# Another order of the same 1100 steps on every engine: gated mix of a long convolution and a token-shift MLP

## The chip, the cores and the metric

The kernel runs on one core of one Trainium2 chip. The metric is the time of one execution on the device in microseconds. Five engines of the core have instruction streams of their own: PE (matmul), DVE (vector), ACT (scalar), POOL (GpSimd) and SP, which here only issues DMAs. Each engine runs its own instructions in the order in which the program gives them; semaphores make an instruction wait for data from another engine or for a buffer to come free.

## The reference

All inputs are bf16; q, k, v are 1 x 2048 x 640, and x is q.

```
a = q * (irfft(rfft(kv, 4096) * rfft(ssm_k, 4096))[:2048] + kv * ssm_D),  kv = k_shift * v
k_shift[s] = sum over t < 4 of k[s - (3 - t)] * shift_k[:, 3 - t] (per channel)
h  = gelu(layernorm(x) @ w1)           # 640 -> 640
hs = shift(h) @ w2                     # four channel groups, moved by +1, -1, +2, -2 tokens
x1 = x + hs
b  = x1 + gelu(layernorm(x1) @ w3) @ w4   # 640 -> 1536 -> 640
g  = sigmoid(sum(x * gate_w))
out = g * a + (1 - g) * b
```

## The kernel before

Tokens are split over 16 tiles of 128 rows. The MLP works in four chunks (c = 0 to 3) of four tiles: `x_stats` and `x_norm` make the layernorm, `x_turn` transposes the chunk (on PE for chunks 0 and 1, by one DMA_TRANSPOSE issued from SP, line 648, for chunks 2 and 3), `mlp1.c.u` (line 703) is five matmuls of 512 columns into one PSUM bank with a gelu on ACT behind them, `h_shift` and `h_tile` move the tokens, `w2` (line 785) adds the second product to x. `x1_norm.c` makes the second layernorm; its step 6 issues the DMA_TRANSPOSE into the tile x1t. `w3.c.f` (line 837) and `w4.t` (line 864) are the wide MLP.

The long convolution is a Fourier transform of 4096 points done as matmuls, both for kv and for ssm_k. `tap` (line 586) makes k_shift on PE; DVE multiplies it with v into KV (lines 598, 601). `step1` (line 419) is the first transform of KV and of the filter (HT0); its results are cast from PSUM to a staging tile `stg` (lines 356 on ACT, 358 on DVE) and stored to DRAM (S_x, S_h; steps 15 and 16 of each step1, line 433). `gather.x.s` and `gather.h.s` (line 440) read them back, permuted, into tiles `ax`; `step2` (line 461) is the second transform, `product` the complex product on DVE, `step3` (line 508) the inverse, stored to S_g and read by `gin`, and `step4` (line 890) the last transform, joined with the gate and with b. `load_h` loads parts of ssm_k, `load_gw` the gate's weights.

PSUM has 8 banks of 2 KB per partition, shared by all these matmuls. A helper's steps can be emitted one by one; the letters in a step's name (as in `step1.KV.3.AAAVAVAAAV:9`) say for each PSUM evacuation whether ACT (A) or DVE (V) does it:

```
    def evac(ev, dst, src):
        if ev == "A":
            A.copy(out=dst, in_=src)
        else:
            V.tensor_copy(out=dst, in_=src)
```

The order of all engines is one list, `ORDER`, of 1100 entries `helper.arguments.engines:k`, and `emit` executes the k-th step of the named helper, inside `tc.manual_schedule`, which keeps the order as given. So each engine's stream is the list cut to what that engine does; SP's stream (some 100 DMA-issuing steps) is cut from the same list, and all its DMAs go into one hardware queue. `SLOTS` gives for each allocation of a shared ring (tag c: the PSUM banks; row, gt, xt, gq, ax, hp: SBUF rings of 3 or 4 tiles, xt of 2) which buffer it takes; an allocation waits until the last user of that buffer is through.

Of the kernel before, what the change touches and what calls it, by code (L numbers as in the profile page):

```python
# [41 lines left out]
def kernel(  # L42
# [24 lines left out]
        "c": "012345670124703510347205142356401723605162370514731057423671045261304732641374153670421350627413"  # L67
             "502634751264351270361427503164257364102546173045621537426107432715604371401362570164301257613045"
             "267236057416537621507362651374026372401534762501373150427102547535706432073125640736450750634127"
             "504763270415367204325170635147630125460327156034215760147362304167135620316425031672301402715320"  # L70
             "1724107361761423564023714053627501267420674256271306234",
        "row": "01230213021302320123012031203120310310303",
        "gt": "012301031010231012301201",
        "xt": "010101",
        "gq": "0120201201021020120122102121021021",
        "ax": "0123120312030213",
        "hp": "01231302",
# [798 lines left out]
    def step4(t1, ev):  # L876
# [26 lines left out]
        def total():  # L903
# [170 lines left out]
                 f1_table=f1_table, t2_table=t2_table, i_tables=i_tables, f4_table=f4_table, kv_alloc=kv_alloc, k_load=k_load, k_wrap=k_wrap, v_load=v_load, tap=tap,  # L1074
# [51 lines left out]
```

## Time and profile before

| | us |
|---|---|
| median of 3 executions | 229.26 |
| lowest, highest | 227.95, 229.72 |
| span of the profiled execution (first to last instruction) | 225.9 |
| PE busy | 217.5 |
| DVE busy | 192.4 |
| ACT busy | 173.0 |
| POOL busy | 16.3 |
| PE's granted clock, mean | 0.999 |

The profile gives no time of its own for the profiled execution beside its span; the median of the three executions stands 3.4 us above that span. In a row of the profile `out<-in` names the tiles, `xN` is the number of instructions, and the figure behind the comma the mean length of one in ns. Rows of a chain or a timeline begin with start and length in us. PE's 217.5 us count each matmul from its start to a modelled end.

### The profile page before, as it was taken

Reading aid. Unit: us, or ns where it says so; the run is one execution under the profiler, and the core shown is the slowest. Engines: PE = TensorE matmul, PEld = TensorE weight load, DVE = VectorE, ACT = ScalarE, POOL = GpSimd, SP = SyncE. Lnnn points to the kernel's source line nnn. Section 1 sums busy time; section 2 is a strip of 40 time slices with the busy share of each in tenths; the row PEclk is TensorE's granted clock in tenths of the full one; section 3 lists DMA queues with packets and bytes.
Section 4 is the critical chain, followed back from the end, with each engine's and each line's share of the span. In section 5 each row is a group of like instructions: output and inputs, shape, how many; then the busy total and the mean of one; then the engine's idle time right before and its main releaser. Section 6 shows DMA issues by size and latency. Waiting matters only on the chain.

```text
span 225.9 us, 6037 instructions
## 1 busy us (share of the span) xinstructions
PE 217.5 (96%) x2419; PEld 120.4 (53%) x2420; DVE 192.4 (85%) x500; ACT 173.0 (77%) x344; POOL 16.3 (7%) x34
## 2 busy tenths in 40 slices
PE   8979989999999999999999999999999999999994
PEld 2557555436846554344664445555533547657762
DVE  7899999999999999873999998989999841439994
ACT  4799988989989989999977597967988450266450
POOL 3238020000000200010400000000000000000000
PEclk9999999999999999999999999999999999999999
DMA  6999997964998999999999560592695779418915
GB/s 238 381 362 336 308 249 193 344 282 104 392 352 353 307 240 290 376 361 369 300 250 303 121 232 4 156 361 70 69 323 195 219 269 372 189 30 321 310 77 197
DMA packets 43841, 57.62 MB, mean 255 GB/s; under 512 B 20514, under 2 KB 36514, under 8 KB 43558
## 3 DMA queue, kind: packets, MB, share of 16 engines
q1 hardware_dynamic: 43238, 54.62, 75.3%
q0 software_dynamic: 576, 2.62, 3.1%
q8 instruction: 19, 0.31, 0.6%
q14 instruction: 8, 0.07, 0.1%
HBM read 34.94 MB, written 18.36 MB: 236 GB/s over the span
## 4 chain that ended last, share of the span: by engine, by line
PE 63%; DMA 16%; DVE 15%; issue 1%; ACT 1%; SPq 1%; ACTq 0%
PE ps L864 23%; PE ps L837 18%; DMA WA<-in_B_w_dram 5%; DMA W<-in_B_w_dram 5%; PE ps L461 4%; PE ps L890 4%; PE psw L785 4%; PE psm L703 4%; DMA ax<-S_x 4%; PE ps L508 3%; DMA S_h<-stg 3%; PE ps L419 2%; DVE KV L601 2%; DVE KV L598 2%; DVE HT L358 2%; DVE HM L758 1%
## 5 line engine op out<-in xcount | busy, mean ns | idle before, releaser
L837 PE MATMUL ps<-x1t,W 128*128 128x512 bf16 x240 | 56.1, 380 | 0.0
L864 PE MATMUL ps<-W,gt 128*128 128x320 bf16 (+2 forms) x383 | 55.1, 299 | 0.6 <-DMA W<-in_B_w_dram 0.5
L864 PEld LDWEIGHTS <-gt 128*128 128x128 bf16 x384 | 36.2, 98 | 18.3 <-issue 2.8
L841 ACT ACTIVATE gt<-ps 128x512 bf16<-128x512 f32 x48 | 27.6, 609 | 19.0 <-PE ps L864 10.6
L837 PEld LDWEIGHTS <-W 128*128 128x128 bf16 x240 | 21.8, 98 | 28.2 <-issue 5.5
L356 ACT CAST stg<-ps 128x512 bf16<-128x512 f32 x55 | 28.6, 608 | 3.0 <-PE ps L419 1.8
L867 DVE SCALAR_TENSOR_TENSOR X<-ps,OMG,X 128x320 bf16<-128x320 f32 (+2 forms) x32 | 17.2, 548 | 11.9 <-PE ps L864 11.7
L703 PE MATMUL psm<-xt,WA 128*128 128x512 bf16 x100 | 23.4, 379 | 1.2 <-DMA WA<-in_B_w_dram 1.1
L356 ACT CAST gs<-ps 128x320 bf16<-128x320 f32 x41 | 15.6, 439 | 8.7 <-PE ps L508 5.2
L785 PE MATMUL psw<-WA,HT 128*128 128x320 bf16 x116 | 21.3, 299 | 0.2
L358 DVE CAST XS<-ps 128x512 bf16<-128x512 f32 x19 | 12.5, 684 | 5.3 <-PE ps L461 5.3
L356 ACT CAST hs<-ps 128x512 bf16<-128x512 f32 x28 | 15.0, 606 | 1.9 <-PE ps L461 1.9
L358 DVE CAST stg<-ps 128x512 bf16<-128x512 f32 x25 | 15.9, 683 | 0.2
L703 PEld LDWEIGHTS <-WA 128*128 128x128 bf16 x100 | 9.2, 97 | 12.0 <-DMA WA<-in_B_w_dram 1.2
L785 PEld LDWEIGHTS <-HT 128*128 128x128 bf16 x116 | 10.9, 98 | 7.7 <-issue 4.1
L894 ACT ACTIVATE y<-ps,GS 128x320 bf16<-128x320 f32 x22 | 10.4, 526 | 5.7 <-PE ps L890 3.5
L788 DVE SCALAR_TENSOR_TENSOR X<-psw,X 128x320 bf16<-128x320 f32 x32 | 14.2, 483 | 0.1
L358 DVE CAST gs<-ps 128x320 bf16<-128x320 f32 x23 | 10.7, 485 | 2.4 <-PE ps L508 1.7
L706 ACT ACTIVATE HT<-psm 128x512 bf16<-128x512 f32 x20 | 11.6, 618 | 1.2 <-PE psm L703 1.1
L356 ACT CAST XS<-ps 128x512 bf16<-128x512 f32 x21 | 11.9, 609 | 0.5 <-PE ps L461 0.3
L785 PE MATMUL psw<-WA,HM 128*128 128x320 bf16 x44 | 12.3, 299 | 0.0
L794 ACT ACTIVATE jk<-X 128x640 bf16<-128x640 bf16 x16 | 12.1, 759 | 0.0
(145 smaller groups left out, 334.8 us busy)
## 6 DMA issues: line engine op xcount, KB each, us to landing
S_x<-stg SPq DMA_DIRECT2D x8, 640.0 KB
S_h<-stg SPq DMA_DIRECT2D x8, 640.0 KB, 3.4
ax<-S_x SPq DMA_DIRECT2D x8, 640.0 KB, 8.1
ax<-S_h SPq DMA_DIRECT2D x8, 640.0 KB, 6.0
S_g<-gs SPq DMA_DIRECT2D x8, 640.0 KB, 3.6
W<-in_B_w_dram SPq DMA_DIRECT2D x2, 1920.0 KB
kn<-in_A_k_dram SPq DMA_DIRECT2D x4, 640.0 KB
E<-in_A_ssm_k_dram SPq DMA_DIRECT2D x5, 512.0 KB
```

The costliest lines, as they stand in the source:

```text
L356: A.copy(out=dst, in_=src)
L358: V.tensor_copy(out=dst, in_=src)
L703: PE.matmul(ps[:].rearrange("p (a b) -> p a b", a=4), lhsT=W1N[:, k, 160 * u:160 * u + P] if u < 4 else W1M[:, k, :], rhs=xt[:, :, k, :], ...
L706: A.activation(out=st["HT"][:, 4 * c:4 * c + 4, u, :], in_=ps[:].rearrange("p (t b) -> p t b", t=4), func=ACT.Gelu_apprx_tanh)
L785: PE.matmul(ps[:], lhsT=h_tile(f, t1), rhs=W2P[:, f, o:o + W], start=(f == 0), stop=(f == 4))
L788: V.scalar_tensor_tensor(out=X1[:, t1, o:o + W], in0=box["ps"][:], scalar=1.0, in1=X[:, t1, o:o + W], op0=ALU.mult, op1=ALU.add, accum_out ...
L794: A.activation(out=jk[:], in_=X1[:, t1, :], func=ACT.Square, accum_out=S12[:, 1, t1:t1 + 1])
L837: PE.matmul(ps[:].rearrange("p (a b) -> p a b", a=4), lhsT=st["W3"][:, k, f * P:(f + 1) * P], rhs=xt[:, :, k, :], start=(k == 0), stop=(k ...
L841: A.activation(out=st["gt", c, f // 4][:, f % 4, :], in_=ps[:], func=ACT.Gelu_apprx_tanh)
L864: PE.matmul(ps[:], lhsT=st["gt", c, f // 4][:, f % 4, i * P:(i + 1) * P], rhs=st["W4"][:, f, o:o + w], start=(f == 0), stop=(f == FC - 1))
L867: V.scalar_tensor_tensor(out=X1[:, t1, o:o + w], in0=box["ps"][:], scalar=OMG[:, t1:t1 + 1], in1=X1[:, t1, o:o + w], op0=ALU.mult, op1=ALU ...
L894: A.activation(out=box["y"][:], in_=box["ps"][:], func=ACT.Copy, scale=GS[:, t1:t1 + 1])
```

## The change

`ORDER` and `SLOTS` are replaced. The new list has the same 1100 steps, and the functions are unchanged. What differs is the order of the steps on every engine, SP's DMAs among them; the letters of 13 kinds of helper (for instance step1 of KV 27 A and 13 V before, 28 and 12 after; step2.x 21 and 19, then 24 and 16; step3 41 and 23, then 47 and 17; step4 22 and 10, then 18 and 14; x1_norm 6 and 10, then 4 and 12); and the buffer of each ring allocation. Of the ORDER part only lines with steps that are spoken of below are shown.

```
 
     SLOTS = {
-        "c": "012345670124703510347205142356401723605162370514731057423671045261304732641374153670421350627413"
-             "502634751264351270361427503164257364102546173045621537426107432715604371401362570164301257613045"
-             "267236057416537621507362651374026372401534762501373150427102547535706432073125640736450750634127"
-             "504763270415367204325170635147630125460327156034215760147362304167135620316425031672301402715320"
-             "1724107361761423564023714053627501267420674256271306234",
-        "row": "01230213021302320123012031203120310310303",
-        "gt": "012301031010231012301201",
-        "xt": "010101",
-        "gq": "0120201201021020120122102121021021",
-        "ax": "0123120312030213",
-        "hp": "01231302",
+        "c": "012320145673270641524072103647534126427016104237162507437023645136502746354127057402136401357106"
+             "425302745643750173654120350314267513254062045163704376510246135640172306537062145302153674315647"
+             "021573204612071646023754256473017436520705126343625710471235120734653140302037541671403515146730"
+             "203764154176364715207256413501267412104673540721631524075162727270653672451610237161617024172037"
+             "2061401020273030712031264056170261340360431746012350450",
+        "gt": "001110203320201301201302",
+        "row": "00123133312013021320132320302021231021013",
+        "xt": "011101",
+        "gq": "010020110012022012201201021",
+        "ax": "0123130213022301",
+        "hp": "01232031",
     }
     taken = {}
 
@@ -906,169 +906,175 @@
...
-        "k_load.3.AVA:2 load_x.3:0 x_norm.0.VVAA:2 x_stats.1.VVVV:1 k_load.3.AVA:3 x_turn.0.AAA:0 k_load.3.AVA:6 "
-        "k_load.2.VAV:5 load_w1.1:0 x_norm.0.VVAA:3 k_load.2.VAV:1 x_stats.1.VVVV:2 x_turn.0.AAA:1 x_stats.1.VVVV:3 "
...
-        "x_norm.3.VVVV:0 x_norm.3.VVVV:1 k_load.0.AAV:4 load_cj:0 k_load.0.AAV:2 mlp1.1.2:1 x_norm.3.VVVV:2 "
...
-        "mlp1.1.4:0 x_turn.3.D:0 kv_consts:0 x_stats.2.VVAA:2 mlp1.1.0:0 k_load.2.VAV:2 k_wrap:0 k_load.1.AVV:6 "
...
-        "tap.3.VAVA:7 z_cols:0 mlp1.1.1:1 load_gw:0 tap.4.VAAV:5 tap.4.VAAV:3 mlp1.3.1:0 tap.3.VAVA:2 x_stats.2.VVAA:7 "
...
-        "x_turn.2.D:0 h_shift.3:0 tap.0.AVAA:0 tap.2.AVAA:3 tap.2.AVAA:7 tap.2.AVAA:5 tap.3.VAVA:8 mlp1.3.3:0 "
...
-        "mlp1.3.2:1 load_h.1:0 mlp1.2.2:0 tap.0.AVAA:8 tap.2.AVAA:1 tap.1.VAVA:7 h_shift.1:1 tap.0.AVAA:2 load_h.3:0 "
...
-        "step2.x.3.AVVVVVAAVA:8 load_w4:0 w3.0.1:1 scale_x1.4.V:0 step2.x.0.VAVVAVAAVA:12 w3.0.2:1 w3.0.8:1 "
...
-        "step2.x.0.VAVVAVAAVA:4 step2.x.3.AVVVVVAAVA:13 gather.h.6:0 step2.x.0.VAVVAVAAVA:13 x1_norm.1.VVAA:4 "
...
-        "w4.3:2 step2.h.3.AAVVVVAVAA:2 x1_norm.1.VVAA:6 scale_x1.2.A:0 step2.h.3.AAVVVVAVAA:7 step2.h.3.AAVVVVAVAA:8 "
...
-        "w3.1.5:0 w3.1.6:0 step2.h.0.AAVAAAAAVA:10 step2.h.0.AAVAAAAAVA:11 step2.h.0.AAVAAAAAVA:5 step3.7.AAAAAVAV:0 "
...
-        "gather.x.2:0 x1_norm.2.AVVV:4 w4.0:2 w3.1.5:1 w3.1.9:0 x1_norm.2.AVVV:5 w3.1.2:1 product.1:3 product.1:4 "
...
-        "x1_norm.3.AVAA:2 w3.1.3:0 scale_x1.11.A:0 step3.1.VAAVVVAA:6 w3.1.0:0 x1_norm.2.AVVV:6 w3.1.10:0 "
...
...
+        "load_w1.1:0 mlp1.0.2:0 x_norm.1.VVVA:0 x_norm.1.VVVA:1 x_turn.1.VVA:0 x_norm.1.VVVA:2 load_x.3:0 "
...
+        "x_stats.3.VVAA:7 x_norm.3.VVVV:0 mlp1.1.3:1 x_norm.3.VVVV:1 x_norm.3.VVVV:2 x_norm.3.VVVV:3 x_turn.3.D:0 "
...
+        "tap.3.VVVA:4 x_stats.2.VVAA:4 x_stats.2.VVAA:5 tap.3.VVVA:8 tap.3.VVVA:6 mlp1.3.0:0 mlp1.3.0:1 "
...
+        "tap.1.AAVV:2 x_turn.2.D:0 load_h.4:0 step1.KV.3.VAVAVAAAVV:11 tap.1.AAVV:3 z_cols:1 z_cols:2 tap.1.AAVV:6 "
+        "tap.1.AAVV:4 step1.KV.3.VAVAVAAAVV:10 mlp1.2.4:0 mlp1.2.4:1 h_shift.0:1 h_shift.0:2 load_w2:0 mlp1.2.0:0 "
...
+        "step2.x.0.AVAVVVAAVV:0 load_w4:0 step2.x.0.AVAVVVAAVV:2 step2.x.3.VAVVAAAAVA:0 step2.x.3.VAVVAAAAVA:7 "
...
+        "step2.h.3.VVVVAAVAVA:13 gather.h.6:0 step2.h.3.VVVVAAVAVA:9 step2.h.3.VVVVAAVAVA:11 "
...
+        "step2.h.0.AAAAAAAAAV:2 product.7:0 w2.14:4 step2.h.0.AAAAAAAAAV:5 product.7:1 product.7:2 pow0:0 w4.2:3 "
+        "product.7:3 step2.h.0.AAAAAAAAAV:1 gather.x.2:0 product.7:4 gather.h.3:0 w4.3:0 step2.h.0.AAAAAAAAAV:11 "
...
+        "step3.7.AAVAAAAA:2 step3.7.AAVAAAAA:3 product.1:0 product.1:1 product.1:2 product.1:3 x1_norm.1.VVVV:6 "
+        "w3.1.0:0 step3.7.AAVAAAAA:1 w3.1.0:1 step3.7.AAVAAAAA:5 w3.1.8:0 product.1:4 step3.7.AAVAAAAA:9 "
...
+        "x1_norm.2.VVVA:5 gather.x.3:0 step2.x.1.AAAVAAVAAA:12 step2.x.1.AAAVAAVAAA:6 product.0:0 "
...
+        "w3.1.7:0 w3.1.7:1 x1_norm.2.VVVA:6 w3.2.2:0 w3.2.2:1 step2.h.1.AAVVAAAVVA:6 step2.h.1.AAVVAAAVVA:7 "
...
```

306 rows, old and new, of the table ORDER are left out of this document.

## The prediction

> **What bounds the kernel now.** I read the page first, for the shares.
>
> ```profile
> span 225.9 us, 6037 instructions
> PE 217.5 (96%) x2419; PEld 120.4 (53%) x2420; DVE 192.4 (85%) x500; ACT 173.0 (77%) x344; POOL 16.3 (7%) x34
> ```
>
> PE is busy for 217.5 of 225.9 us. The change keeps every PE instruction, so it can win no more than PE's 8.4 us of idle time, and lose as much as it likes. The windows of 10 us show where those 8.4 us lie (columns: PE, PEld, DVE, ACT, POOL busy, granted clock, DMA share, GB/s).
>
> ```profile
> 0.00:10.00 10.00, 8.92 (x38) 3.75 (x39) 7.88 (x41) 5.65 (x9) 3.53 (x15) 1.00 0.80 303
> 10.00:20.00 10.00, 8.22 (x87) 5.51 (x85) 9.65 (x31) 9.95 (x18) 4.28 (x5) 1.00 1.06 354
> 20.00:30.00 10.00, 9.52 (x186) 6.22 (x187) 9.44 (x35) 9.99 (x21) 2.32 (x4) 1.00 1.00 289
> 30.00:40.00 10.00, 9.77 (x262) 5.66 (x252) 9.60 (x36) 8.00 (x17) 1.32 (x2) 1.00 0.87 238
> 40.00:50.00 10.00, 9.42 (x127) 3.66 (x116) 9.52 (x27) 8.94 (x18) 0.00 (x0) 1.00 0.80 302
> 60.00:70.00 10.00, 9.69 (x71) 5.00 (x68) 9.84 (x30) 9.13 (x16) 0.00 (x0) 1.00 0.95 365
> 100.00:110.00 10.00, 9.49 (x84) 5.29 (x85) 5.69 (x16) 9.84 (x24) 0.52 (x1) 1.00 1.06 368
> 110.00:120.00 10.00, 10.00 (x182) 6.23 (x181) 9.41 (x19) 8.49 (x15) 1.89 (x4) 1.00 1.13 257
> 180.00:190.00 10.00, 10.00 (x88) 5.46 (x87) 3.78 (x9) 2.88 (x6) 0.00 (x0) 1.00 0.85 309
> 220.00:226.00 6.00, 2.75 (x22) 1.52 (x20) 2.77 (x7) 0.00 (x0) 0.00 (x0) 0.95 0.54 200
> ```
>
> PE's idle time is 1.1 us in the first window, 1.8 in the second, 2.1 in the five others shown up to 110 us, and 3.25 behind 220, the tail. From 110 on PE is full. DVE is at 9.4 to 9.8 of 10 in the windows of 10 to 70 us: there PE runs at the pace at which DVE empties PSUM and builds operands. After 110 us a new order can win nothing in PE, only lose.
>
> The chain that ended last says the same (start us, length us, what): a weight load, DVE work in the first half, a DMA of W4, then PE alone.
>
> ```profile
> 3.55 11.11 DMA WA<-in_B_w_dram
> 14.65 0.05 issue
> 14.70 3.41 PE psm L703 x15
> ...
> 43.56 0.34 DVE KV L598
> 43.94 0.61 PE ps L419 x4
> 44.55 1.19 PE psm L703 x5
> ...
> 94.93 10.73 DMA W<-in_B_w_dram
> 105.66 0.05 issue
> 105.71 5.06 PE ps L864 x36
> ...
> 222.12 1.02 DVE X L867 x2
> ```
>
> **The change part by part.** Steps, instructions and DMAs are the same; four things move.
>
> *Engines of the evacuations.* The prices:
>
> ```profile
> L356 ACT CAST stg<-ps 128x512 bf16<-128x512 f32 x55 | 28.6, 608 | 3.0 <-PE ps L419 1.8
> L358 DVE CAST stg<-ps 128x512 bf16<-128x512 f32 x25 | 15.9, 683 | 0.2
> L356 ACT CAST gs<-ps 128x320 bf16<-128x320 f32 x41 | 15.6, 439 | 8.7 <-PE ps L508 5.2
> L358 DVE CAST gs<-ps 128x320 bf16<-128x320 f32 x23 | 10.7, 485 | 2.4 <-PE ps L508 1.7
> ```
>
> Counting the letters in the step names, step1 and step2 send 4 casts of 512 columns from DVE to ACT (step1 +1 and +1, step2.x +3, step2.h -1): DVE -4 x 0.683 = -2.7 us, ACT +4 x 0.608 = +2.4. step3 sends 6 casts of 320 columns: DVE -6 x 0.485 = -2.9, ACT +6 x 0.439 = +2.6. The small moves in the taps, norms, transposes and step4 go both ways and stay under 2 us per engine in sum. DVE thus loses some 5 us of work and ACT gains some 3. The step3 part lies where PE is full (after 110 us): worth nothing. The 512-column part lies where DVE sets the pace.
>
> To say what it is worth I add up, in list order and with the durations of rows like these, the work of each engine ahead of every PE step, and take the largest amount by which the DVE work it needs exceeds PE's own: that much PE must stand idle. In the first 100 us this lead is 7.9 us before (at step2.x.3) and 5.0 after. So the DVE-paced stalls should shrink by 7.9 - 5.0 = **2.9 us**. The rows allow it only just: idle PE between 10 and 110 us is about 3.9 (1.8 + 2.1), plus slow spots between kinds that busy time hides. I take -2.9 and keep 0 as the other end.
>
> *Start.* On SP's queue the loads went k.3, x.1, k.2, x.3, w1.1, w1.0; now k.0 and k.1 stand ahead of w1.1, and x.3 behind it. w1.1, which landed at 14.65, thus has one 640 KB load more ahead of it, about 1.85 us at the 354 GB/s of the window 10 to 20; I take 1.6, as it is issued a little earlier. x.3 comes later by more than that. PE has 1.9 us more of k and x transposes listed ahead of the first mlp1 step, which fill that wait. Sum 0; the ends are +1.6 (nothing hides it) and -1.1 (PE's only long wait for a weight goes):
>
> ```profile
> PE psm L703 <- DMA WA<-in_B_w_dram: 1.1, 1, 1.1
> PE ps L864 <- DMA W<-in_B_w_dram: 0.5, 1, 0.5
> ```
>
> *The two DMA transposes of the first layernorm* (x_turn.3.D and x_turn.2.D). The last normalising run ahead of the first of them (from the chain; it ends at 24.16), the issue times, and the first matmuls that need chunk 2:
>
> ```profile
> 23.00 1.16 DVE xn L660 x3
> 24.18 3.43 SPq L648 DMA_TRANSPOSE xt<-xn  x1
> 34.45 2.81 SPq L648 DMA_TRANSPOSE xt<-xn  x1
> ```
> ```profile
> 30.77 4.48 PE L703 MATMUL psm<-xt,WA 128*128 128x512 bf16 x20
> 40.72 2.33 PE L703 MATMUL psm<-xt,WA 128*128 128x512 bf16 x10
> ```
>
> No row gives their landing. The bounds: not before the issue itself is through (2.81 and 3.43 us), and not after the first use (40.72 - 34.45 = 6.3 us). Like sizes in the list of DMA issues (KB, median us to landing) lie between:
>
> ```profile
> S_h<-stg SPq DMA_DIRECT2D x8, 640.0 KB, 3.4
> ax<-S_x SPq DMA_DIRECT2D x8, 640.0 KB, 8.1
> ax<-S_h SPq DMA_DIRECT2D x8, 640.0 KB, 6.0
> ```
>
> I take 5.6, near the 6.0 row, since the queue is full there (DMA share 1.00 and 0.87). For chunk 3 the last x_norm moves 1.6 to 2.7 us later on DVE (1.6 us more DVE work stands ahead of it, and its x arrives later), so the issue moves to about 26.9 and the landing to 32.3. The first step that reads it, mlp1.3.0, has 2.1 us less PE work ahead of it than mlp1.3.1 had; PE gets there at about 30.4. Stall 1.9 (ends 0 and 3.7). For chunk 2, the DVE work ahead is 0.4 us more and its first reader, mlp1.2.4, stands 2.0 us of PE work earlier; PE is 1.9 late by then, DVE partly too, since its taps wait for PE's: stall 1.4 (ends 0 and 2). Also load_h.1, load_h.2, gate weights and load_h.0 are now issued ahead of that transpose. Behind each waiting mlp1 step on PE stand the tap matmuls that feed DVE, so DVE loses the time as well. Sum of both: **+3.3 us** (0 to 5.7).
>
> [...]
>
> *Second half.* PE's list changes kind 6 times more often after 110 us; a change of kind costs about 0.07 us, worked out from the chain's rows:
>
> ```profile
> 120.29 2.16 PE ps L837 x10
> 122.45 0.41 PE ps L508 x16
> 122.86 2.26 PE ps L837 x10
> ```
>
> (2.26 against 2.16 for the same ten matmuls is 0.1 at a change.) That is +0.4 us (0 to 0.6). Three transfers get less cover. gather.h.6 is issued behind step2.x.0's first step, which leaves PE 3.9 us of work before its reader, where the rows above have 3.4 to 6.0 for this size; at their middle, 4.7, and with 0.3 of changes of kind between, +0.5 us (0 to 2.1). x1_norm.1's transpose of the second layernorm (tile x1t) now stands on SP behind gather.x.2 and gather.h.3, which wait until step2.h.3 has freed their buffers, though the data is ready long before; its landing and its first reader, w3.1.0, come out at the same time: +0.3 (0 to 2). x1_norm.2's stands behind gather.x.3 in the same way: +0.3 (0 to 1). Together **+1.5 us** (0 to 5.7). Nothing hides these: PE is full there and its queue is in order. If SP waits, what it has queued behind (the later gathers) is late too. This is the queue's row:
>
> ```profile
> SPq L440 <- PE ps L461: 22.5, 5, 11.0
> ```
>
> *Tail.* After PE's last matmul the same steps follow as before, so the 3.25 us stay. [...]
>
> **Sum:** 0 (start) + 3.3 - 2.9 + 1.5 = +1.9 us. The profiled execution shows a span of 225.9; the median of the three runs, 229.26, is 3.4 above it, and I take those 3.4 us outside the span as unchanged. So 229.26 + 1.9 = **231.2 us**. The case's own range takes ±1.5 to 2: 229.3 to 232.6.
>
> **The rivals.**
>
> *1. The new waits compound.* One SP queue carries everything; each late wait holds back what is queued behind it, and step1.HT0.0's staging reuses the buffer of HT0.1, whose store stands behind two gathers, so ACT may stop there too. Upper halves of the bounds: early 4.2, second half 2.8, DVE-paced gain 2.9: +4.1, 233.3. For: the 22.5 us that SP's queue already waits in the row above. Against: ACT has 1 to 2 us of slack per window at 30 to 50 us.
>
> *2. Other side: the DVE relief stays and the transposes are early enough.* It is one mechanism: x_norm.3's chain keeps its place in time (DVE's lead at the start is smaller too), and the transposes land in 3.4 us as the S_h store does. Then chunk 3 lands at 26.9 + 3.4 = 30.3, ahead of PE's 30.4, the early stall is at most 0.5, the second half costs the 0.4 of switches, and the sum is 0.5 - 2.9 + 0.4 = -2.0: 227.3. It decides at a landing within 3.5 us of issue, or an issue before 24.8. For: DVE really sheds its casts in the windows where it is at 9.6. Against: the queue is fuller there than where the 3.4 was measured.
>
> *3. Nothing to be measured.* PE is 96% busy, DVE takes back what the early stalls give: sum 0, 229.3.
>
> **How the numbers follow.** Forecast 0.45, rival 1 0.25, rival 2 0.20, rival 3 0.10. One per cent of 229.26 is 2.3 us, about what a measurement of this kernel can tell from no change. Faster by that needs under 227.0: the lower half of rival 2 and a little beside, 0.13. Slower needs over 231.6: nearly all of rival 1 and four tenths of the forecast, 0.43. Within: 0.44. The range runs from rival 2's time to above rival 1's with its ends, 227.0 to 236.0; what is left out below and above is about 2 in 10.
>
> **What would show it.** In the changed kernel's windows, PE's idle time in 20 to 50 us should grow to about 4.6 from 1.3, with a wait of psm (L703) for the DMA of xt; in 50 to 105 us it should nearly vanish; W4's wait may go. After 110 us windows with PE below 9.9 and waits of ps for ax or x1t would be the second-half term. I am wrong if PE never waits for xt (then the transposes land sooner, or DVE reaches x_norm sooner), if DVE still holds PE between 50 and 100 us (the lead is not what costs), or if PE waits after 110 us come to more than 3 us (then the single DMA queue is the bound, not my early stall).

## The result

The changed kernel takes **235.81 us** (median of 4 executions, 234.96 to 237.49) where the kernel before takes 228.91 in the same comparison (median of 4, 227.95 to 229.72): a ratio of **1.0299, interval 1.0223 to 1.0375**. That is 6.9 us slower, on the side that had the chance 0.43, and 4.6 us above the predicted 231.2. It lies within the range of 227.0 to 236.0, by 0.2 us. Some executions of either kernel take several us longer than its others; the ratios leave out those that lie more than 1.5% above the quickest of the same kernel. The profiled execution took 235.12 us.

The page of the changed kernel, shares first:

```profile
span 233.4 us, 6034 instructions
PE 219.6 (94%) x2419; PEld 121.2 (52%) x2420; DVE 190.0 (81%) x488; ACT 175.9 (75%) x349; POOL 16.9 (7%) x34
```

PE has its 2419 matmuls as before, DVE and ACT the shares that the new letters give them (190.0 against 192.4, 175.9 against 173.0). The span is 7.5 us longer: PE's idle time went from 8.4 to 13.8 us, and its busy time from 217.5 to 219.6 for the same work.

Windows by stage tell where. First the kernel before, then the changed one (columns: PE, PEld, DVE, ACT, POOL busy, granted clock, DMA share, GB/s):

```profile
2.00:20.00 18.00, 16.14 (x120) 8.83 (x118) 16.54 (x63) 14.34 (x26) 6.61 (x10) 1.00 1.02 363
20.00:50.00 30.00, 28.70 (x540) 15.54 (x538) 28.56 (x94) 26.93 (x53) 3.64 (x6) 1.00 0.89 276
50.00:105.00 55.00, 54.46 (x497) 29.67 (x495) 48.51 (x148) 52.49 (x106) 2.41 (x4) 1.00 0.93 314
105.00:160.00 55.00, 54.49 (x747) 30.01 (x731) 51.05 (x90) 44.45 (x91) 2.41 (x4) 1.00 0.68 200
```
```profile
2.00:20.00 18.00, 17.60 (x155) 10.83 (x153) 16.71 (x61) 15.51 (x27) 5.68 (x9) 1.00 1.02 380
20.00:50.00 30.00, 25.14 (x491) 12.66 (x489) 25.16 (x75) 25.49 (x51) 3.58 (x5) 1.00 0.85 250
50.00:105.00 55.00, 53.91 (x437) 30.11 (x437) 49.01 (x161) 52.32 (x100) 3.47 (x6) 1.00 0.88 309
105.00:160.00 55.00, 52.15 (x733) 27.05 (x732) 45.64 (x82) 44.32 (x99) 2.93 (x4) 1.00 0.68 190
```

PE's idle time falls by 1.5 us in the first stage (1.86 to 0.40) and grows by 3.6 in the second (1.30 to 4.86), by 0.6 in the third (0.54 to 1.09), by 2.3 in the fourth (0.51 to 2.85). DVE loses as much as PE in 20 to 50 us (28.56 to 25.16 busy). From 160 to 220 us nearly nothing changes (0.07 to 0.34). So there are two places, 20 to 50 and 105 to 160 us.

Idle time by the clock mixes lateness with the order of the work. I therefore also add up PE's own work in list order, with the durations of the rows, and take it from the time at which PE gets there. This lateness is reckoned from the rows and is itself no row. By amount of PE work done:

| PE work done, us | 20 | 35 | 55 | 90 | 125 | 200 |
|---|---|---|---|---|---|---|
| late before, us | 3.8 | 5.6 | 8.7 | 12.5 | 14.5 | 16.9 |
| late after, us | 3.6 | 9.6 | 12.9 | 15.7 | 21.3 | 24.3 |
| difference | -0.2 | +4.0 | +4.2 | +3.2 | +6.8 | +7.4 |

Four us are lost by PE work 35, one comes back by 90, and four more are lost by 200.

What PE waits for in the changed kernel (us in total, times, longest):

```profile
PE psm L703 <- DMA xt<-xn: 3.0, 2, 2.5
PE ps L837 <- ACT gs L356: 1.6, 1, 1.6
...
PE psk L586 <- issue: 0.8, 1, 0.8
PE ps L461 <- DMA ax<-S_h: 0.7, 1, 0.7
...
PE ps L837 <- DMA x1t<-xn: 0.2, 1, 0.2
```

None of these five stood in the profile before. The first is the wait that the prediction named; the chain gives its two transfers, from issue to landing, and PE's timeline what stands behind them:

```profile
25.76 6.04 DMA xt<-xn
...
36.92 5.76 DMA xt<-xn
...
108.71 7.48 DMA ax<-S_h
...
116.85 8.09 DMA x1t<-xn
```
```profile
31.84 1.25 PE L703 MATMUL psm<-xt,WA 128*128 128x512 bf16 x5 [2.46 <-DMA xt<-xn]
...
38.04 0.43 PE L586 MATMUL psk<-DG,KT 32*128 32x128 bf16 x23 [0.85 <-issue]
...
42.73 2.33 PE L703 MATMUL psm<-xt,WA 128*128 128x512 bf16 x10 [0.54 <-DMA xt<-xn]
```

x_turn.3.D lands at 25.76 + 6.04 = 31.80 and mlp1.3.0 starts at 31.84, after 2.46 us of nothing on PE; mlp1.2.4 waits 0.54 for x_turn.2.D.

DVE has two long stops between 20 and 46 us that the prediction did not list (from its waits in that window):

```profile
DVE KV L601 <- DMA KV<-in_A_v_dram,ROWS: 1.8, 1, 1.8
DVE KV L601 <- PE psk L586: 1.7, 1, 1.7
```

The second is the echo of PE's late taps. The first is for a load of v that had not landed yet. GpSimd's timeline shows it, before and then after:

```profile
20.06 0.94 POOL L172 DMA_INDIRECT KV<-in_A_v_dram,ROWS  x1 [0.30 <-issue]
21.02 1.05 POOL L653 TENSOR_TENSOR RS<-VE,EXPO 128x4 f32<-128x4 f32 x1
```
```profile
18.04 0.94 POOL L172 DMA_INDIRECT KV<-in_A_v_dram,ROWS  x1 [0.30 <-issue]
...
21.95 1.04 POOL L653 TENSOR_TENSOR RS<-VE,EXPO 128x4 f32<-128x4 f32 x1 [2.97 <-DVE VE L691]
23.52 1.02 POOL L172 DMA_INDIRECT KV<-in_A_v_dram,ROWS  x1 [0.16 <-issue]
```

Before, the fourth load of v went out at 20.06, ahead of the power step of x_stats.3 (L653). The new list puts that load, `v_load.2:0`, behind the power step, which waits 2.97 us for DVE; so it goes out at 23.52, 3.5 us later, and DVE stops for it.

In the second half the 1.6 us is a buffer. The timelines of ACT and of SP's queue:

```profile
136.41 0.44 ACT L356 CAST gs<-ps 128x320 bf16<-128x320 f32 x1
142.44 0.75 ACT L356 CAST gs<-ps 128x320 bf16<-128x320 f32 x2 [1.84 <-DMA S_g<-gs]
```
```profile
136.88 0.36 SPq L519 DMA_DIRECT2D S_g<-gs  x1
138.40 4.20 SPq L818 DMA_TRANSPOSE x1t<-xn  x1
```

`SLOTS` gives step3.6's output tile gs the row buffer 0, which step3.1's gs has. Its store goes out at 136.88 and lets go of the buffer at 142.4, so ACT waits 1.84 us and w3.1.7 on PE 1.6 us for the bank that ACT should empty. x1_norm.2's transpose stands directly behind that store on SP.

### The profile page after: what moved, and what is told of

The parts are those of the page before. It is cut to its first block, busy times and chain, and to the rows that moved or that the text cites. A ratio compares the mean times of both kernels' runs of the same rounds, so it can differ in the third digit from the quotient of the medians.

```text
span 233.4 us, 6034 instructions
## 1 busy us (share of the span) xinstructions
PE 219.6 (94%) x2419; PEld 121.2 (52%) x2420; DVE 190.0 (81%) x488; ACT 175.9 (75%) x349; POOL 16.9 (7%) x34
## 4 chain that ended last, share of the span: by engine, by line
PE 41%; DMA 19%; ACT 16%; DVE 13%; issue 4%; DVEq 0%; ACTq 0%
PE ps L837 15%; PE ps L864 10%; DMA x1t<-xn 9%; DMA xt<-xn 5%; PE psw L785 5%; ACT stg L356 4%; DMA ax<-S_h 3%; DVE X L904 3%; PE ps L461 3%; PE psm L703 3%; ACT jk L794 2%; DVE q L900 2%; PE ps L508 2%; DVE q L897 2%; PE ps L419 2%
## 5 line engine op out<-in xcount | busy, mean ns | idle before, releaser
L864 PE MATMUL ps<-W,gt 128*128 128x320 bf16 (+2 forms) x383 | 55.8, 299 | 0.1
L356 ACT CAST stg<-ps 128x512 bf16<-128x512 f32 x57 | 30.2, 610 | 2.9 <-DMA S_h<-stg 1.2
L356 ACT CAST gs<-ps 128x320 bf16<-128x320 f32 x47 | 17.8, 439 | 11.5 <-PE ps L508 8.4
L358 DVE CAST stg<-ps 128x512 bf16<-128x512 f32 x23 | 15.0, 686 | 1.8 <-PE ps L419 1.1
L788 DVE SCALAR_TENSOR_TENSOR X<-psw,X 128x320 bf16<-128x320 f32 x32 | 14.7, 485 | 1.0 <-PE psw L785 0.7
L894 ACT ACTIVATE y<-ps,GS 128x320 bf16<-128x320 f32 x18 | 8.7, 527 | 7.0 <-PE ps L890 4.7
L461 PE MATMUL ps<-ax,CMP 64*32 64x256 bf16 (+3 forms) x512 | 12.6, 299 | 1.2 <-DMA ax<-S_h 0.7
L356 ACT CAST XS<-ps 128x512 bf16<-128x512 f32 x24 | 13.4, 620 | 0.5 <-PE ps L461 0.4
L358 DVE CAST gs<-ps 128x320 bf16<-128x320 f32 x17 | 8.0, 485 | 5.4 <-issue 3.1
L794 ACT ACTIVATE jk<-X 128x640 bf16<-128x640 bf16 x16 | 12.3, 768 | 0.1
L486 DVE TENSOR_TENSOR XS<-XS,hs 128x2560 bf16<-128x2560 bf16 x8 | 11.9, 1489 | 0.2
```

Source lines behind the costliest of these rows:

```text
L461: PE.matmul(ps[j][q:q + 32, lo - 512 * u:hi - 512 * u], lhsT=CMP[HALF[j], 8 * b + 4 * h + i, c, :], rhs=st[name, 2 * b + h][HALF[j], i, lo ...
L486: V.tensor_tensor(out=x, in0=x, in1=h, op=ALU.mult)
L788: V.scalar_tensor_tensor(out=X1[:, t1, o:o + W], in0=box["ps"][:], scalar=1.0, in1=X[:, t1, o:o + W], op0=ALU.mult, op1=ALU.add, accum_out ...
L794: A.activation(out=jk[:], in_=X1[:, t1, :], func=ACT.Square, accum_out=S12[:, 1, t1:t1 + 1])
L864: PE.matmul(ps[:], lhsT=st["gt", c, f // 4][:, f % 4, i * P:(i + 1) * P], rhs=st["W4"][:, f, o:o + w], start=(f == 0), stop=(f == FC - 1))
```

## The experiments

The theory ahead of the runs was that each named wait costs its length and gives it back when what it waits for comes earlier. The rival was that on in-order queues the next wait takes its place. The diffs show the edited steps or digits alone; each edit is made to the changed kernel unless it says otherwise. Ratios are to the kernel before on the same chip; the comparisons were made on several chips, so ratios are what may be compared between them. Idle times of PE by stage are in a table behind the runs.

**Another row buffer for step3.6.**

```diff
-        "row": "00123133312013021320132320302021231021013",
+        "row": "00123133312013021320132320302120231021013",
```

> The changed kernel with one edit in the row ring: gs.6 (staging of step3.6) takes buffer 1 and gs.0 buffer 0, where they took 0 and 1. Theory A (two waits in a row, each able to hold PE alone): the 1.8 us in which ACT stands before gs.6's first cast, waiting for the S_g store of gs.1, goes, but PE then stands at w3.2.2 for x1_norm.2's transpose, which lands at 144.7 whatever ACT does: gain 0.4 us (0.1 to 0.8). Rival B: the slot wait is the whole cost at 142 us: gain 1.8 to 2.2 us.

Measured: 236.44 us, 1.0405 (1.0362 to 1.0449). No gain. In the profiled execution the wait of 1.6 us at w3.1.7 for ACT is gone, and w3.2.2, which waits 0.2 us in the changed kernel's row above, waits 1.8 for its x1t. That execution had also lost 3.6 us at w3.1.0 before; the next run has the same edit in it and shows the same shift, smaller, without that.

**The buffer, and x1_norm.2's steps earlier.**

```diff
+ (behind x1_norm.2.VVVA:2)   x1_norm.2.VVVA:3 x1_norm.2.VVVA:4 x1_norm.2.VVVA:5
- (behind w3.1.10:1, w3.1.6:0 and step3.1.VAAAAAVA:7)   the same three
```

> e1 and, besides, the three last normalising steps of x1_norm.2 moved up to right behind its second step (ahead of product.6 on DVE, ahead of some gelu and cast steps on ACT); its DMA keeps its place on SP. Theory A: the transpose is issued about 3 us earlier, PE waits neither at w3.1.7 nor at w3.2.2, gain 2.0 us (1.5 to 2.5) against the changed kernel, much more than the slot alone. Rival B: it gains no more than e1, because ACT and DVE, full there, are late by what was moved ahead of their other work.

Measured: 236.62 us, 1.0415 (1.0372 to 1.0459). No gain again. PE's waits in 105 to 160 us and SP's queue:

```profile
PE ps L837 <- DMA x1t<-xn: 1.5, 2, 1.0
PE ps L461 <- DMA ax<-S_h: 1.4, 1, 1.4
PE ps L837 <- ACT gs L356: 0.6, 1, 0.6
```
```profile
138.51 0.36 SPq L519 DMA_DIRECT2D S_g<-gs  x1
138.92 4.32 SPq L818 DMA_TRANSPOSE x1t<-xn  x1
```

The data of the transpose is ready earlier, but on SP the store of step3.1 still stands ahead of it and goes out at 138.51; the transpose follows at 138.92, no earlier than the 138.40 of the changed kernel. The wait for gs falls from 1.6 to 0.6 us, the one for x1t rises from 0.2 to 1.5, the one for the gather from 0.7 to 1.4. The rival's outcome came, but not for its reason (ACT and DVE late): the place is SP's queue.

**mlp1 in another order, so that PE doesn't need x_turn.3.D first.** Twelve mlp1 steps change places:

```diff
- mlp1: 3.0 3.4 3.1 3.2 1.1 2.4 2.0 2.3 2.1 3.3 2.2 1.0
+ mlp1: 1.1 1.0 3.4 3.1 3.0 3.2 2.4 3.3 2.3 2.1 2.0 2.2
```

> The changed kernel with the twelve mlp1 steps of the stretch from 29 to 56 us permuted among their own places, so that mlp1.1.1 and mlp1.1.0, which need no DMA transpose, come before the first mlp1.3, and chunk 2 comes last. Buffers and all else as in the changed kernel. Theory A (the early waits for the two transposes carry to the end): PE's wait of 3.0 us for xt goes, DVE's two stops of 1.8 us behind it too, and the time falls by 2.5 to 3.5 us. Rival B (another engine paces PE until 95 us anyway): the wait goes, but the gain is given back before 95 us; time falls by less than 1 us.

Measured: 236.43 us, 1.0392 (1.0341 to 1.0442). No gain. PE's waits between 20 and 46 us:

```profile
PE psk L586 <- issue: 1.9, 1, 1.9
PE psm L703 <- DVE KV L601: 1.2, 1, 1.2
```

The wait for xt is gone. At the same place mlp1 now waits 1.2 us for a PSUM bank that DVE's KV step, itself late for v, has not freed, and the pause put down to "issue" grows from 0.8 to 1.9 us. PE's idle time in 20 to 50 us is 30.0 - 25.17 = 4.83, against 4.86.

**All three edits together.**

```diff
+ the row buffers, the x1_norm.2 steps and the mlp1 order of the three runs above
```

> e2 and e3 together. If the early waits and the ones at 142 us are separate and both carry to the end (theory A of each), the gains add: 4.5 to 5.7 us under the changed kernel, 230 to 231 us, still 1 to 2 us above before. If the early gain is given back (rival), the time falls by 2 to 2.5 us only.

Measured: 239.62 us, 1.0523 (1.0483 to 1.0562): slower than the changed kernel. PE's timeline and a window of 4 us:

```profile
129.80 2.31 PE L837 MATMUL ps<-x1t,W 128*128 128x512 bf16 x5 [3.60 <-DVE XS L486]
```
```profile
128.00:132.00 4.00, 2.20 (x5) 0.58 (x5) 3.72 (x7) 0.00 (x0) 0.00 (x0) 0.65 0.90 313
```

PE stops for 3.60 us ahead of w3.1.0, the first reader of x1_norm.1's transpose, which goes out on SP at 119.39 here and at 116.85 in the changed kernel. The row names a DVE step as releaser, but by the semaphore's updates in the trace the transpose has landed at 129.75, 0.05 us ahead of the matmul; in the repeat of the changed kernel, next, the row of the same step names the transpose, with 0.04 us between. Behind the pause the clock is cut (the 0.65 is the mean of these 4 us), and the five matmuls that take 1.25 us elsewhere take 2.31.

**The changed kernel once more.**

```diff
  (no edit)
```

> The changed kernel itself, as the control for the runs beside it: 235.8 as before, with a wait at w3.1.0 (first reader of the second x1t) that is 0.2 us in one execution and 1.4 to 3.7 in others of its variants, by when that transpose lands.

Measured: 237.61 us (234.04 to 240.18), 1.0335 (1.0243 to 1.0428), in agreement with the first comparison. Its executions spread over 6 us, those of the kernel before over 4.3 in this comparison and 1.8 in the first. The profiled execution has a wait at w3.1.0 that the first profile doesn't have:

```profile
PE ps L837 <- DMA x1t<-xn: 3.6, 2, 3.4
```

x1_norm.1's transpose goes out at 119.00 here and takes 10.17 us to landing, where it went out at 116.85 and took 8.09. So the 3.60 us of the run above need not come from its edits: the changed kernel has this wait itself, from nothing to 3.4 us.

**The load of v early.**

```diff
  v_load.0:0
+ v_load.2:0
...
  tap.4.VAVA:0
- v_load.2:0
```

> The changed kernel with one step moved: v_load.2, the last of the four indirect loads of v on GpSimd's queue, ahead of x_stats.3's power step instead of behind it. Theory A (the load of v held DVE): DVE's wait of 1.8 us for KV at 28 us goes, but PE still waits for the first transpose until 31.8: PE's position at 31.8 us is the same, total gain 0 to 1 us. Rival B (the v load alone is the early loss): PE's wait at mlp1.3.0 goes too, gain 2.5 to 3.5 us.

Measured: 233.84 us, 1.0303 (1.0237 to 1.0369). By the times alone it can't be told from the changed kernel. The traces do tell it. GpSimd's timeline, DVE's wait for v in 20 to 46 us, and the window:

```profile
19.48 0.94 POOL L172 DMA_INDIRECT KV<-in_A_v_dram,ROWS  x1 [0.31 <-issue]
```
```profile
DVE KV L601 <- DMA KV<-in_A_v_dram,ROWS: 0.2, 1, 0.2
```
```profile
20.00:50.00 30.00, 26.38 (x501) 13.23 (x499) 25.96 (x76) 26.80 (x53) 2.94 (x5) 1.00 0.87 265
```

The load goes out at 19.48 instead of 23.52, DVE's wait for it falls from 1.8 to 0.2, and PE's idle time in this stage from 4.86 to 3.62. PE's wait for xt falls too, from 3.0 to 1.9 us: x_turn.3.D takes 4.83 us from issue to landing in place of 6.04 when the load of v no longer runs beside it. This holds in every profile of the changed kernel and its variants: 4.29 to 5.12 us in the five with the load early, 6.02 to 6.30 in the eight with it late. The span is 230.4 against 233.4. So the load of v has a part in the early loss of some 1.2 us.

**The load of v and the mlp1 order.**

```diff
+ v_load.2:0 behind v_load.0:0, and the mlp1 order above
```

> e2 and e5 together: mlp1 steps permuted and v_load.2 early. Theory A (two covers over one place, each hid the other): neither bank nor transpose is late at 29 us, PE's wait there goes as a whole, gain at 35 us of PE's own work 2.3 to 3 us, in the time 1.5 to 3 us against the control. Rival B (a third limit, for instance DVE's own work, holds PE there): less than 1 us.

Measured: 235.53 us, 1.0348 (1.0308 to 1.0387); span 233.0. No wait for xt is left, yet PE's idle time in 20 to 50 us is 3.61, as with the load of v alone: an "issue" pause of 2.0 us stands there instead, and the third stage loses 1.0 us more. The order of mlp1 is no cure.

**Both transposes of the second layernorm earlier on SP.** To the buffer and the x1_norm.2 steps is added:

```diff
  gather.h.0:0
+ x1_norm.1.VVVV:6
...
- x1_norm.1.VVVV:6
  w3.1.0:0
...
  gather.x.3:0
+ x1_norm.2.VVVA:6
...
  w3.1.7:1
- x1_norm.2.VVVA:6
```

> The changed kernel with e3's edits (gs.6 in another buffer, x1_norm.2's last steps early) and both of the second layernorm's transposes earlier on SP's queue: x1_norm.1's right behind gather.h.0 instead of behind gather.x.2 and gather.h.3, x1_norm.2's right behind gather.x.3 instead of behind step3.1's store. Theory A (the order on SP's one queue makes the waits between 115 and 145 us): PE waits at neither w3.1.0, w3.1.7 nor w3.2.2, gain 2 us against the control's quickest executions and more against its median, and the spread of the times gets smaller. Rival B (the gathers that are now behind it come late instead): gain under 1 us, with new waits of ps for ax.

Measured: 233.58 us (233.11 to 234.69), 1.0275 (1.0230 to 1.0321). SP's queue and the window:

```profile
133.42 2.60 SPq L818 DMA_TRANSPOSE x1t<-xn  x1
...
137.32 0.36 SPq L519 DMA_DIRECT2D S_g<-gs  x1
```
```profile
105.00:160.00 55.00, 53.63 (x744) 28.09 (x743) 47.46 (x85) 46.30 (x103) 3.70 (x4) 1.00 0.69 201
```

x1_norm.2's transpose is ahead of the store now, goes out 5.0 us earlier (133.42 against 138.40) and lands in 4.12 us (by its semaphore's updates). PE's idle time in the stage falls from 2.85 to 1.37. No wait is left at w3.1.0 and w3.2.2; 0.8 us for the gather and 0.6 for gs remain. The times lie within 1.6 us, as the theory said. The buffer and the x1_norm.2 steps, which gave nothing without SP's place, are part of this; whether the two moved transposes alone would do it was not run.

**Both: the load of v and the transposes.**

```diff
+ v_load.2:0 behind v_load.0:0, and all edits of the run above
```

> e5 and e7 together: v_load.2 early on GpSimd's queue, the two transposes of the second layernorm early on SP's, gs.6 in another row buffer. Theory A (three separate places, each a queue or a buffer, not engine work): the gains of PE's lag add, 2.9 and 1.8 us, so 229.5 to 231.5 us, and still 2 to 3 us above before, for the waits left at 30 to 45 us. Rival B (one of them only moves the wait to the next place): no better than e5 or e7 alone, 233.5 us.

Measured: 232.47 us, 1.0213 (1.0149 to 1.0278). The windows:

```profile
2.00:20.00 18.00, 15.67 (x138) 10.29 (x136) 14.66 (x55) 14.01 (x23) 5.82 (x9) 0.91 1.01 372
20.00:50.00 30.00, 27.16 (x506) 13.93 (x504) 27.41 (x81) 26.87 (x53) 3.50 (x5) 1.00 0.80 257
...
105.00:160.00 55.00, 54.30 (x756) 28.51 (x762) 47.92 (x86) 46.82 (x104) 3.71 (x4) 1.00 0.68 207
```

PE's idle time is 2.84 in the second stage and 0.70 in the fourth: the two cures don't take from one another. The time is still above the 229.5 to 231.5 of theory A, if by 1 us. The first stage lost 1.9 us (2.33 against 0.40), with a clock of 0.91. PE's timeline shows how, and the window behind it:

```profile
8.47 2.27 PE L615 MATMUL pst<-IDB,kn 128*128 128x128 bf16 x20 [2.25 <-DMA kn<-in_A_k_dram]
```
```profile
10.00:12.00 2.00, 2.00 (x12) 1.13 (x10) 1.92 (x6) 2.00 (x3) 0.00 (x0) 0.51 1.00 415
```

k.3 landed late in this execution, PE stood for 2.25 us, and the clock is 0.51 from 10 to 12 us. Nothing of this run's edit stands so early.

**Before's letters for step1 and step2.x on top of that.** Five casts of 512 columns go back from ACT to DVE, to put a price on the DVE relief:

```diff
- step1.KV.3.VAVAVAAAVV, step1.KV.2.VAAAVVAAAV, step1.KV.1.AAVAAAAAAA, ...
+ step1.KV.3.AAAVAVAAAV, step1.KV.2.AVAVAVAAAA, step1.KV.1.VAVAAAVVAA, ...
```

> e8 with the letters of step1 and step2.x of the kernel before, put on the same places in the list: DVE gets 5 casts of 512 columns back from ACT, 3.4 us of work, and some casts change engine both ways. Theory A (DVE paces PE from 35 to 95 us, and the shed work was worth its time, but DVE started it late): the lag of PE at 90 us of its own work grows by 1.5 to 3.4 us and so does the time. Rival B (the shed casts were worth nothing, since DVE was not the limit): within 1 us of e8.

Measured: 254.19 us, span 250.7 in the profile. PE's largest wait between 40 and 70 us:

```profile
PE ps L419 <- ACT stg L356: 3.6, 3, 1.9
```

The run is inconclusive on its question. Each letter moves a cast to another in-order queue at a place that the list chose for the old one, and these waits, 3.6 us in one row alone, swamp 5 x 0.7 us of work. It shows that letters and order belong together, and prices neither.

**More idle matmuls at the start.** The changed kernel has 14 of the 23 warming matmuls ahead of k.3's transposes, the kernel before 20.

```diff
  warm:1
+ warm:2 warm:3 warm:4
...
  k_load.3.AAA:4
- warm:2 warm:3 warm:4
```

> The changed kernel with PE's idle matmuls on zeros (steps warm:2 to warm:4, nine of 23) back ahead of k.3's transposes, where the kernel before has all but three of them; everything else as changed. Theory A (PE meets k.3's landing, which differs by 2 us between executions, with nothing to do, and its clock is cut behind a pause of 2 us or more): no execution shows a granted clock below 1.00 in the first 20 us, and the median falls by 1 to 1.5 us against the changed kernel's 236 to 237. Rival B (the mean clock of 0.991 to 0.993 comes only from the pause at w3.1.0 near 125 us): no change.

Measured: 237.26 us, 1.0329 (1.0245 to 1.0414). No gain, though the first 20 us of the profiled execution show a granted clock of 1.00, as the theory asked: at about 30 us PE still waits for xt, 2.4 us in one piece, and the clock is 0.67 from 32 to 36 us. The theory's 2 us fit the pause of 2.25 us in 'Both', which the 0.51 follows; as a threshold they are not shown: behind 2.46 us in the changed kernel's first profile the clock is 1.00 from 32 to 36 us.

**The same with the load of v and the transposes.**

```diff
+ warm:2 to warm:4 behind warm:1, and all edits of 'Both'
```

> e8 with the same edit. Both places where PE's clock was cut are then gone (k.3's landing, w3.1.0). Theory A: mean granted clock 0.998 to 1.000 in every execution, time 229.5 to 231 us, ratio to the kernel before 1.008 to 1.013. Rival B: as e8, 232.5 us and a clock of 0.992.

Measured: 232.35 us (231.18 to 233.31), 1.0157 (1.0099 to 1.0216), the lowest ratio of the variants and the only one whose interval lies below that of the changed kernel. Its median is that of the run without the warming matmuls (232.47); the ratio is lower since the kernel before is slower in this comparison (229.28 against 227.98). The run just above is on the same chip and differs in the load of v and the transposes with their edits alone: its lowest time, 234.73, lies above the highest here, 233.31, and the medians of the executions that the ratios count are 236.77 and 232.35. So these edits give back 4.4 us. The clock doesn't tell the executions apart: four have a mean of 1.000 and take 231.18 to 233.31 us, two have 0.991 and 0.993 and take 232.06 and 233.24. The profiled one has a pause of 1.75 us for k.2 and a clock of 0.50 from 12 to 14 us. None of the variants beats the kernel before.

PE's idle time by stage in one profiled execution of each, worked out from the windows as above (the first edit and the repeat, whose profiled executions have the long wait at w3.1.0, are left out, as is the run with the old letters):

| | 2-20 | 20-50 | 50-105 | 105-160 | 160-220 | span |
|---|---|---|---|---|---|---|
| before | 1.86 | 1.30 | 0.54 | 0.51 | 0.07 | 225.9 |
| changed | 0.40 | 4.86 | 1.09 | 2.85 | 0.34 | 233.4 |
| buffer, x1_norm.2 steps | 1.78 | 5.07 | 0.84 | 3.66 | 0.00 | 233.5 |
| mlp1 order | 0.53 | 4.83 | 1.45 | 2.82 | 0.00 | 233.2 |
| these together | 0.83 | 4.85 | 2.48 | 6.65 | 0.15 | 239.9 |
| load of v | 1.48 | 3.62 | 0.92 | 1.92 | 0.00 | 230.4 |
| load of v, mlp1 order | 1.96 | 3.61 | 1.92 | 2.38 | 0.00 | 233.0 |
| transposes on SP | 0.66 | 4.81 | 1.09 | 1.37 | 0.24 | 231.5 |
| load of v, transposes | 2.33 | 2.84 | 0.93 | 0.70 | 0.00 | 230.1 |
| warm | 1.66 | 4.22 | 1.27 | 2.84 | 0.28 | 234.9 |
| warm, load of v, transposes | 2.74 | 3.31 | 1.00 | 0.84 | 0.00 | 230.3 |

## Why the prediction was right, and where it was not

*What bounds it.* "It can win no more than PE's 8.4 us of idle time, and lose as much as it likes", and after 110 us it "can win nothing in PE, only lose", held: the loss sits in waits, not in work.

*Start, 0.* Right as a sum: PE is 0.2 us less late at PE work 20 (3.6 against 3.8). The 1.5 us less idle time of the first stage belongs to this one execution: in the variants with the same start this stage idles between 0.53 and 1.78 us.

*The two DMA transposes, +3.3.* Right in place and near in size, the size in part by luck: +4.0 us by PE work 35. The issue was put at 26.9 and the landing at 32.3, and they came at 25.76 and 31.80; the taken 5.6 us to landing measured 6.04 and 5.76. The stalls were put at 1.9 and 1.4 and measured 2.46 and 0.54, 3.0 in sum; the pause of 0.85 us put down to "issue", which the prediction doesn't have, makes up most of the rest of the 4.0. What the step missed is the load of v on GpSimd's queue: it followed the moved steps past SP's queue, and none past GpSimd's. The run with the load of v early shows its part: 4.86 to 3.62 us of PE's idle time, and a landing sooner by 1.2.

*The DVE relief, -2.9.* **This is the step that failed.** The lateness shows about 1 us given back between PE work 55 and 90 (+4.2 to +3.2), and PE's idle time in 50 to 105 us grew from 0.54 to 1.09 where the prediction said that it "should nearly vanish". The 2.9 us came from a lead that was counted in list order, and in the kernel before PE hardly waited for DVE. Between 10 and 110 us its waits for DVE were these two:

```profile
PE ps L419 <- DVE KV L598: 0.6, 1, 0.6
...
PE ps L419 <- DVE X L788: 0.2, 1, 0.2
```

That is 0.8 us. The 3.9 us of idle time that were said to allow the term "only just" hold 1.1 and 0.7 us of waits for the loads of w1 and k, 0.5 for W4 and 0.5 for ACT, which fewer casts on DVE can't shorten. In the changed kernel PE waits for DVE once between 50 and 100 us, 0.48 us at 58.64; so the prediction's sign of being wrong "if DVE still holds PE between 50 and 100 us (the lead is not what costs)" is met, by little.

A count tells the rest; it fits, but no run isolates it. DVE's lead did become smaller, as counted. But the lead is to be added to how late DVE itself is, and I added it to nothing. At PE work 55, DVE, reckoned in the same way, was late by 2.9 us before and by 7.7 after, since the early stalls stopped it as well (1.8 us for v, 1.7 for PE's taps). 7.7 + 5.0 = 12.7 us is about PE's lateness there, 12.9; before it was 3.4 + 7.9 = 11.3 at its step, where PE was 12.3 late, so that DVE was 1.0 us ahead and did not hold it. By this count the relief was spent on the same engine's lateness. The prediction's own sentence "DVE loses the time as well" was written and not carried into the sum: the two terms were taken as independent. The size of the relief by itself stays unmeasured; the run with the old letters could not price it.

The letters also put work on ACT. From 76 to 99 us the chain of the changed kernel runs on ACT, but for one store of 4.13 us and short pieces; before, it has two DMAs of 6.1 and 8.1 us there:

```profile
76.39 0.45 ACT jk L794 x2
...
98.45 0.60 ACT gt L841
```

PE's waits for ACT between 50 and 105 us come to 0.2 us, so what this cost, if anything, is not shown.

*Second half, +1.5.* The mechanisms are there, mis-sized: +4.2 us between PE work 90 and 200 (+3.2 to +7.4). Of the three transfers with less cover, a gather makes PE wait 0.7 us (0.5 was said), though at step2.h.0 and not at gather.h.6's reader. (For gather.h.6 the middle of 3.4 and 6.0 us was taken; the row of its own kind, `ax<-S_h`, was the 6.0.) x1_norm.1's transpose lands at 124.94, just as its reader gets there, and costs nothing in the profiled execution (0.3 was said, 0 to 2), but 3.4 us in that of the repeat and 3.60 in that of one variant. x1_norm.2's costs 0.2 us behind another wait, and 1.8 and 1.0 in the runs in which that wait is gone or shorter. The missing entry is this other wait, 1.6 us for the row buffer that step3.6 takes over from step3.1. I had followed the row ring only at step1.HT0.0, where ACT does wait, 1.2 us:

```profile
L356 ACT CAST stg<-ps 128x512 bf16<-128x512 f32 x57 | 30.2, 610 | 2.9 <-DMA S_h<-stg 1.2 <-PE ps L419 1.1 <-DMA xt<-xn 0.4
```

and which leaves PE 0.2 us of waiting. The prediction would call itself wrong "if PE waits after 110 us come to more than 3 us (then the single DMA queue is the bound...)". By the rows they come to 1.6 + 0.7 + 0.2 = 2.5 us in the first profile, so that line was not crossed there; in the repeat's they come to 5.4. The reading behind the line was right: the edits that moved transposes ahead of what SP holds gained, and those that only made their data ready earlier did not. The rest of the 4.2 us, some 1.7, has no wait to its name: six more changes of kind on PE, at the predicted 0.07 us, would be 0.4 of it, and what the other 1.3 are is open.

*The sum.* 0 + 4.0 - 1.0 + 4.2 = 7.2 us, about the 7.4 of the table and the 7.5 of the span, against the predicted 0 + 3.3 - 2.9 + 1.5 = 1.9. That the time stayed inside the range, by 0.2 us, is owed to the width of the range and not to the sum.

*The rivals.* Rival 1, waits that compound on the one SP queue, came nearer than the forecast: its early 4.2 is what was measured (4.0). Its second half, 2.8, is too small, and it kept the 2.9 of relief. Rival 2 asked for a landing within 3.5 us of issue, or an issue before 24.8; they were 6.04 and 25.76. Rival 3's argument, that DVE "takes back what the early stalls give", has it the wrong way round by the count above: the early stalls took back what DVE's letters gave.

*Left open.* The variant with the lowest ratio is still 1.6% above the kernel before. Its profile has PE waits for xt of 1.2 us, an "issue" pause of 0.9 and 2.7 us for k at the start; these were not taken apart.

## What to carry to other kernels

Before a lead counted in list order is priced as a gain, look for it among the waits of the profile: what an engine doesn't wait for can't be won back. When a new order delays one engine early and relieves it later, don't add the two terms as if they were independent: by the count here the relief first has to pay for the lateness of the very engine that it relieves. Follow each moved step past every queue, GpSimd's too, and each ring buffer to the store that last reads it. A transpose whose data is ready earlier gained nothing here while the in-order queue still had a waiting store ahead of it (it went out at 138.92 us against 138.40); move the issue, not the data.

## What the runs showed of the hardware

**Behind pauses of PE of 1.75 to 3.60 us its granted clock was 0.50 in some cases and 1.00 in others.** The traces record the granted clock. Behind a pause of 2.25 us (load of v and transposes), one of 2.44 (warming matmuls), one of 3.60 (all three edits) and one of 1.75 with 0.92 shortly before it (the last run), it is 0.50 for some 3.4 us, worked out from the means of the windows: in the first of these 0.64 from 8 to 10 us and 0.51 from 10 to 12, so (0.36 + 0.49) x 2 / 0.5 = 3.4. Five matmuls take up to 2.31 us there instead of 1.25. Behind 2.46 us in the changed kernel's first profile nothing happens: the five matmuls take 1.25, and the clock is 1.00 from 32 to 36 us. The repeat has both in one execution: behind 2.73 us five matmuls take 2.31, with a clock of 0.60 from 32 to 36 us; at its wait of 3.4 us for x1t the clock of the page's slices stays at 0.9 or more. In the profiled execution before, no wait of PE exceeds 1.1 us. What decides between the two is not shown. The cut cost a good us beyond the wait with all three edits and in the repeat (2.31 - 1.25 = 1.06 in five matmuls); whether it is part of the wide spread of the changed kernel is not shown.

**DMA transposes of one size took from 4.12 to 10.17 us to landing**: 4.12 us in a run in which it goes out ahead of the store, 4.29 to 5.12 and 6.02 to 6.30 us for one and the same transfer without and with a load of v from GpSimd beside it, 8.09 and 10.17 behind two gathers in two executions of the same kernel. The issue holds SP between 2.54 us (x_turn.2.D in the changed kernel's profile) and 7.89 us (in the run with the transposes earlier).

**PE has pauses that no wait explains.** The row "issue" stands in front of a tap matmul with 0.4 us (load of v) to 2.0 us (load of v, mlp1 order), and it grew where the wait in front of it went, from 0.85 to 1.90 us (mlp1 order). The trace of the changed kernel shows one thing beside it: of the packets of 16 KB on the DMA queue that the profile calls "instruction", one runs from 35.56 to 36.44 us, and PE goes on at 38.04, 1.60 us later. What PE waits for there is not shown.
